# Attention with a channel mix on one core: the low parts of the weights subtracted on VectorE instead of GpSimd

## The chip, the cores and the metric

One core of one Trainium2 chip runs the whole program. The metric is the device time of one execution, in microseconds. Engines are named as in the profile: PE (TensorE matmul), PEld (its weight load), DVE (VectorE), ACT (ScalarE), POOL (GpSimd), SP (SyncE, which issues the loads and stores here).

## The reference

Four sequences of 768 tokens with 8 heads of 64 pass through attention with a window of 96 local and 8 global keys and a distance bias; its output, 512 wide, goes through a channel mix:

```python
xk = mu_k * x + (1.0 - mu_k) * x_prev      # x_prev: the token before
xr = mu_r * x + (1.0 - mu_r) * x_prev
k = np.maximum(xk @ w_k, 0.0)              # 512 x 1024
v = k * k @ w_v                            # 1024 x 512
r = 1.0 / (1.0 + np.exp(-(xr @ w_r)))      # 512 x 512
return (r * v).astype(np.float32)
```

The weights come as float64.

## The kernel before

The 3072 tokens are 24 tiles of 128 queries, and 12 chunks of two tiles. For each tile, attention runs in four pairs of heads: `scores` (PE s, L287 for the first seven tiles, L289 and L290 later; then DVE e with the bias and its extreme nmax, L295; ACT exp, L296; DVE r, L302 and L303; POOL e times r, L306), `transposes` (PE t, L317; ACT et, L318) and `weighted` (PE av, L334). The channel mix of a chunk begins three tiles after the chunk's first: `mix` makes xk and xr, each as a high and a low part (POOL or ACT, then DVE L358, ACT L359, DVE L360); then come the products kp with w_k (four banks of 24 matmuls), z with w_r (two of 12) and vps with w_v (two of 24), each as three products of high and low parts (L371 to L373). ACT and DVE square the positive part of kp in between (L397 to L400: kk, kk_hi, kk_lo); ACT makes the sigmoid of z (L405) and DVE multiplies it with vps (L414).

The weights are converted once, at the start, in 20 blocks of 128 x 512: eight of w_k, four of w_r, eight of w_v, in this order (numbers 0 to 19). `weight_begin` loads a block's float64 words (SP, L159) and builds its leading bits as a float32 `a`: ACT Abs (L166 or L169), POOL L167 for the first eight and DVE L170 for the rest, and DVE L171, L172, L173 for all. L174 rounds `a` to the high part hi, on ACT or, for every other pair of blocks, on POOL (whose copies have line L196). `weight_end` subtracts hi from `a`, which gives the low part lo (L180, on POOL). `a` lies in a buffer that a later block, a kk or a sig takes once the subtraction has read it.

Three things set the order. In the source, the tiles are woven with steps of the channel mix by a budget (L423 to L472), and the blocks are begun and ended by a count of slots (L463 to L466). Then the program is built with a scheduler that lays each engine's queue out ahead of time by a timeline of its own (L635), so a change on one engine can move rows on all. On the chip each engine runs its queue in order and waits only where a row's inputs or buffers aren't there. The PSUM banks of kp, z and vps are three (L80), taken in turn: kp, kp, kp, kp, z, z, vps, vps of a chunk, then the next chunk's; each waits until what reads the bank three before it is done. So the second kp of chunk 1 (kp_1270 below) waits for L414 of the first vps of chunk 0 (vps_1072). The pool `p4k` of three buffers (L67) holds the words of blocks 8 to 19, the mixes' sums, and the queries and keys of tiles from 7 on.

Of the kernel before, what the change touches and what calls it, by code (L numbers as in the profile page):

```python
# [9 lines left out]
F32 = mybir.dt.float32  # L10
# [9 lines left out]
B, H, S, D = 4, 8, 768, 64  # L20
# [1 line left out]
NT = S // 128  # L22
NTILES = B * NT
NCHUNK = NTILES // 2
NATIVE = 7  # first tiles, whose scores are plain float32 products
GMAX = 32
LMAX = 97
NEG = -1.0e9
FAR = 1.0e12
HUGE = (1.875 - 2.0**-13) * 2.0**32  # bits 0x4FEFFC00  # L30


@with_exitstack
def tile_biased_attention_channel_mix(ctx: ExitStack, tc: tile.TileContext, qT, kT, v, n_sizes, mu_kr, w_k, w_v, w_r, q_rows, k_rows, v_rows, slopes, out):
    nc = tc.nc
    vec, act, pool, pe = nc.vector, nc.scalar, nc.gpsimd, nc.tensor

    const = ctx.enter_context(tc.tile_pool(name="const", bufs=1))

# [1 line left out]
    sizes_w = const.tile([128, 2, 2], I32, name="sizes_w")  # L41
    nc.sync.dma_start(sizes_w.rearrange("p s w -> p (s w)"), n_sizes.partition_broadcast(128))
    words = const.tile([128, 2, 2], F32, name="words")
    sizes = const.tile([128, 2], F32, name="sizes")
# [13 lines left out]
    nc.scalar.dma_start(mus.rearrange("p a j -> p (a j)"), mu_kr)  # L58
    mu = {name: (mus[:, i, :], mus1[:, i, :]) for i, name in enumerate("kr")}

# [1 line left out]
    wts = {}  # L62
    for name, kts, n in (("k", 4, DF), ("r", 4, DM), ("v", 8, DM)):
        wts[name] = tuple(const.tile([128, kts, n], F32R, name=f"w{name}_{p}") for p in ("hi", "lo"))
# [14 lines left out]
    ps_a = fast.enter_context(tc.tile_pool(name="ps_a", bufs=1, space=PSUM))  # L79
    ps_f = fast.enter_context(tc.tile_pool(name="ps_f", bufs=3, space=PSUM))  # L80

    # the tensor engine's clock rises with use: products of zeros until the first tile is there
    zeros = const.tile([128, 512], BF16, name="zeros")
    vec.memset(zeros, 0.0)
    for i in range(10):
        idle = ps_f.tile([128, 512], F32, name="idle", tag="f")
        pe.matmul(idle, zeros[:, 0:128], zeros, start=True, stop=True)

# [1 line left out]
    # The distance; n_local for a key that is only global, which is over any distance of a local key;  # L90
    # FAR or more where masked: such a key's weight is exactly 0.
    pat = const.tile([128, H, 256], BF16, name="pat")
    pat0 = const.tile([128, H, 128], BF16, name="pat0")
    btmp = f_pool.tile([128, 2048], F32, name="btmp", tag="kk_hi")
# [7 lines left out]
    ints, flts, local, glo, dist0, dist = (piece() for _ in range(6))  # L102
    ints = ints.bitcast(I32)
    j = flts[:, 224:352]
    # 96 keys before the tile, then the tile's own
    pool.iota(ints[:, 96:224], [[-1, 128]], base=0, channel_multiplier=1)
    pool.iota(ints[:, 224:352], [[1, 128]], base=0, channel_multiplier=0)
    pool.iota(ints[:, 0:96], [[-1, 96]], base=96, channel_multiplier=1)
# [3 lines left out]
    vec.tensor_max(causal, causal, dist0)  # L112
    read_sizes()

    # tile 0
    vec.tensor_scalar(local[:, 96:224], causal, nlf, FAR, op0=ALU.is_ge, op1=ALU.mult)
    vec.tensor_scalar(glo, j, ngf, FAR, op0=ALU.is_ge, op1=ALU.mult)
    vec.tensor_add(local[:, 96:224], local[:, 96:224], causal)
# [5 lines left out]
        else:  # L124
            pool.tensor_scalar(pat0[:, h, :], dist0, c, 1.0, op0=ALU.mult, op1=ALU.mult)

    # later tiles: 32 keys from the start, 96 keys before the tile, the tile
    vec.tensor_scalar(local[:, 0:96], flts[:, 0:96], nlf, FAR, op0=ALU.is_ge, op1=ALU.mult)
    vec.tensor_copy(dist[:, 128:256], local[:, 96:224])
    vec.tensor_scalar(dist[:, 0:32], glo[:, 0:32], nlf, None, op0=ALU.max)  # L130
# [11 lines left out]
    w_live = {}  # L142

    def weight_begin(i):
        # A float64 weight's words: (sign, 11 exponent bits, 20 bits), (32 bits).
        # a: its first 24 significant bits as a float32; hi: a rounded to float32r; lo: the rest of a.
        name, src, k, c = w_steps[i]
        if name != "k":
            raw = p4k.tile([128, 512, 2], I32, tag="t4k", name=f"w64_{i}")
            a = f2_pool.tile([128, 512], I32, tag="f2", name=f"wa_{i}")  # L150
        elif k < 2:
            both = f_pool.tile([128, 2048], I32, tag=("kk_hi", "kk_lo")[k], name=f"w64_{i}")
            raw = both[:, 0:1024].rearrange("p (n w) -> p n w", w=2)
            a = both[:, 1024:1536]
        else:
            t = "xk" if k == 2 else "xr"
            raw = f_pool.tile([128, 512, 2], I32, tag=t + "_hi", name=f"w64_{i}")
            a = f_pool.tile([128, 512], I32, tag=t + "_lo", name=f"wa_{i}")
        nc.sync.dma_start(raw.rearrange("p n w -> p (n w)"), src[k * 128 : (k + 1) * 128, 2 * c : 2 * c + 1024])  # L159
        low, top = raw[:, :, 0], raw[:, :, 1]  # L160
        hi = wts[name][0][:, k, c : c + 512]
        # top's bits as a float32: times 2**-112 (or 2**16, which differs in a bit that the shift drops) moves the float64
        # exponent's bias to the float32's. What float32 cannot hold is bounded: from 2**128 up (by Inf, which stays Inf,
        # or the min) to a large number, under 2**-127 (by underflow or the max) to 0.
        if i < 8:
            act.activation(a.bitcast(F32), top.bitcast(F32), AF.Abs, scale=2.0**111)  # L166
            pool.tensor_scalar(a.bitcast(F32), a.bitcast(F32), 2.0**-112, 2.0**-111, op0=ALU.mult, op1=ALU.mult)  # L167
        else:
            act.activation(a.bitcast(F32), top.bitcast(F32), AF.Abs, scale=2.0**16)  # L169
            vec.tensor_scalar(a.bitcast(F32), a.bitcast(F32), 2.0, HUGE, op0=ALU.max, op1=ALU.min)  # L170
        vec.tensor_scalar(a, a, 3, 0x7FFFFFF8, op0=ALU.logical_shift_left, op1=ALU.bitwise_and)  # L171
        vec.scalar_tensor_tensor(a, top, -0x80000000, a, op0=ALU.bitwise_and, op1=ALU.bitwise_or)  # L172
        vec.scalar_tensor_tensor(a, low, 29, a, op0=ALU.logical_shift_right, op1=ALU.bitwise_or)  # L173
        (act.copy if i % 4 < 2 else pool_copy)(hi, a.bitcast(F32))  # L174
        w_live[i] = a

    def weight_end(i):
        name, src, k, c = w_steps[i]
        hi, lo = (w[:, k, c : c + 512] for w in wts[name])
        pool.tensor_sub(lo, w_live.pop(i).bitcast(F32), hi)  # L180

    w_count = [0, 0]

# [11 lines left out]
    def pool_copy(dst, src):  # L195
        pool.tensor_scalar(dst, src, 1.0, 1.0, op0=ALU.mult, op1=ALU.mult)  # L196

# [1 line left out]
    state = {}  # L199
    # the first tiles' queries and keys, with 64 rows of zeros: products of all 128 rows keep the tensor engine's clock up  # L200
    padded = []
    for i in range(2):
        qz = q_pool.tile([128, H, 128], F32, name=f"qz_{i}", tag="qh")
# [5 lines left out]
    def load_tile(n):  # L209
        b, t = divmod(n, NT)  # L210
        s = state[n] = {}
        native = n < NATIVE
        halves = (0,) if native else (0, 64)
        if native:
            qr, kr = padded[n % 2]
        else:
            qr = p4k.tile([128, H, 128], F32, tag="t4k", name=f"qraw_{n}")
            if n == NATIVE:
                kr = kw_pool.tile([128, H, 256], F32, tag="kw", name=f"kraw_{n}")
# [4 lines left out]
        for o in halves:  # L224
            if n <= NATIVE:
                nc.sync.dma_start(kr[o : o + 64, :, 128:256], kT[n])
# [13 lines left out]
        state[n]["va"] = va  # L240

    def global_v(n):
        # the tile before, now with the 32 first rows in place of its own
        b, t = divmod(n, NT)
        if t >= 2:
            nc.sync.dma_start(state[n - 1]["va"][0:32], v[b, 0:32, :])

    def split_tile(n):
# [4 lines left out]
        s["e"] = {}  # L253
        if n < NATIVE:
            return
        qh = q_pool.tile([128, H, 128], F32R, name=f"qh_{n}", tag="qh")
        ql = q_pool.tile([128, H, 128], F32R, name=f"ql_{n}", tag="ql")
        kw = kw_pool.tile([128, H, 256], F32R, name=f"kw_{n}", tag="kw")
        cur = kw[:, :, 0 if n == NATIVE and t else 128 : 256]
        kr = s["kr"]  # L260
        if n == NATIVE:
            kr = kr[:, :, 256 - cur.shape[2] : 256]
# [81 lines left out]
            xt = state["x", c]  # L344
            act.copy(xt[:, :, 1 + 128 * i : 129 + 128 * i], s["av"].rearrange("p (a q) -> p a q", a=4))

# [1 line left out]
    def mix(xc, xp, tag, tmp_pool, out_pool, on_act=False):  # L348
        m, m1 = mu[tag]
        tmp = tmp_pool.tile([128, 4, 256], F32, name=f"mix_{tag}", tag="t4k")  # L350
# [69 lines left out]
        xr = mix(xt[:, :, 1:257], xt[:, :, 0:256], "r", p4k, f_pool, c == 0)  # L420
        return channel_mix(xk, xr, lambda i: out[(2 * c + i) * 128 : (2 * c + i + 1) * 128, :], f_pool, f2_pool, ps_f)

# [1 line left out]
    LAG = 3  # tiles from a chunk's first to the start of its channel mix  # L424
    queue = []
    budget = [0.0]

# [13 lines left out]
    for step in range(NTILES + 1):  # L441
# [4 lines left out]
        for hp in range(4):  # L446
# [8 lines left out]
            if hp == 0:  # L455
                if step >= LAG and (step - LAG) % 2 == 0:
                    queue.append(ffn((step - LAG) // 2))
                    if len(queue) == 1 and step == LAG:
                        budget[0] = -17.5
# [12 lines left out]
        run_ffn(1.0)  # L472
    fast.close()

# [1 line left out]
    def wide():  # L476
        with ExitStack() as g:
            once = g.enter_context(tc.tile_pool(name="g_once", bufs=1))
# [7 lines left out]
            dist, keep = ([once.tile([128, S], F32, name=f"{n}_{t}") for t in range(NT)] for n in ("dist", "keep"))  # L486
# [9 lines left out]
            for t in range(NT):  # L496
                pool.iota(ji, [[-1, S]], base=t * 128, channel_multiplier=1)
                vec.tensor_copy(rel, ji)
                loc = keep[t]
                vec.tensor_scalar(loc, rel, 0.0, None, op0=ALU.is_ge)  # L500
                vec.tensor_scalar(tmp, rel, nlf, None, op0=ALU.is_lt)
                vec.tensor_mul(loc, loc, tmp)
                # only global: n_local; else the distance
                vec.tensor_sub(tmp, glob, loc)
                vec.tensor_scalar(tmp, tmp, 0.0, None, op0=ALU.max)
                vec.tensor_scalar(keep_n, tmp, nlf, None, op0=ALU.mult)
                vec.tensor_scalar(tmp, tmp, -1.0, 1.0, op0=ALU.mult, op1=ALU.add)
                vec.scalar_tensor_tensor(dist[t], rel, -1.0, rel, op0=ALU.mult, op1=ALU.max)
                vec.tensor_mul(dist[t], dist[t], tmp)
                vec.tensor_add(dist[t], dist[t], keep_n)  # L510
                vec.tensor_max(keep[t], loc, glob)
# [49 lines left out]
            rows = xs.rearrange("(b a p) s -> b p a s", b=B, p=128)  # L561
# [16 lines left out]
                    for _ in channel_mix(xk, xr, out_rows, work, work4, ps_f):  # L578
                        pass

    # 1 where the short windows do not hold every kept key
    okf = const.tile([128, 2], F32, name="okf")
    wide_i = const.tile([1, 1], I32, name="wide_i")
    vec.tensor_scalar(okf[:, 0:1], nlf, float(LMAX), None, op0=ALU.is_le)
# [54 lines left out]
```

## Time and profile before

| | |
|---|---|
| median of 3 runs | 525.55 us (525.51 to 526.01) |
| span of the profiled execution | 524.1 us |
| median less span | 1.45 us |
| PE busy | 495.9 us (95%) |
| DVE, ACT, POOL busy | 372.4, 323.6, 283.0 us |

The span is from the first to the last instruction of the one execution that the profiler took; its own time isn't given apart from the span, and the runs' median stands 1.45 us above it. Rows of the timeline begin with a start and a duration in us; in brackets stands how long the engine had been idle and what released it. Rows of groups end with busy time, the mean of one in ns, and the idle time ahead of them. Matmul rows overlap one another, so a matmul's cost is read from start to start.

### The profile page before, as it was taken

How to read it: one execution, taken by the hardware profiler on the slowest of the kernel's cores; microseconds unless marked ns; L12 is line 12 of the kernel's file. 1: busy time of each engine (PE TensorE's matmuls, PEld its weight loads, DVE VectorE, ACT ScalarE, POOL GpSimd, SP SyncE). 2: the span in 40 equal slices, each digit the busy share in tenths (PEclk: the TensorE clock that was granted, in tenths of full speed). 3: DMA queues.
4: the chain of work that ended last, by engine and by line, in shares of the span. 5: the costliest groups of instructions: out<-in, count | busy, mean ns of one | idle time of the engine just before them, and what ended most of it. 6: DMA issues, size and time to landing. Idle time of an engine off the chain costs nothing.

```text
span 524.1 us, 9900 instructions
## 1 busy us (share of the span) xinstructions
PE 495.9 (95%) x3466; PEld 427.2 (82%) x3466; DVE 372.4 (71%) x854; ACT 323.6 (62%) x730; POOL 283.0 (54%) x410
## 2 busy tenths in 40 slices
PE   7885888979999999999999999999999999999995
PEld 4563766869898898898898898898898898898984
DVE  6799999987677766767767867767777865535321
ACT  4868585823957856846847757756757667643220
POOL 8799977987355644544547645535547634203000
PEclk9979799999999999999999999999999999999999
DMA  8998268150350530530521431521422210000101
GB/s 197 322 232 198 67 185 188 41 144 20 107 134 6 141 107 5 157 91 8 162 76 38 130 86 34 133 86 59 124 62 66 62 46 26 35 12 2 41 1 44
DMA packets 27304, 48.16 MB, mean 92 GB/s; under 512 B 7216, under 2 KB 13360, under 8 KB 27248
## 3 DMA queue, kind: packets, MB, share of 16 engines
q1 hardware_dynamic: 27104, 47.46, 34.0%
q8 instruction: 29, 0.48, 0.4%
q14 instruction: 27, 0.22, 0.1%
q10 hardware_dynamic: 144, 0.00, 0.0%
HBM read 41.16 MB, written 6.29 MB: 91 GB/s over the span
## 4 chain that ended last, share of the span: by engine, by line
PE 80%; DVE 11%; POOL 5%; issue 3%; DMA 1%; ACT 0%; DVEq 0%; POOLq 0%
PE vps L372 8%; PE vps L373 8%; PE vps L371 8%; PE kp L371 8%; PE kp L373 8%; PE kp L372 8%; PE av L334 7%; PE t L317 6%; PE z L371 4%; PE z L373 4%; PE z L372 4%; PE s L290 3%; PE s L289 3%; POOL e L306 2%; PE s L287 2%
## 5 line engine op out<-in xcount | busy, mean ns | idle before, releaser
L306 POOL TENSOR_SCALAR e<-e,r 128x256 f32<-128x256 f32 (+1 forms) x192 | 106.1, 570 | 137.0 <-DVE r L303 91.9
L371 PE MATMUL kp<-xk_hi,wk_hi 128*128 128x256 f32 x384 | 108.0, 282 | 0.2 <-DVE kk L398 0.2
L373 PE MATMUL kp<-xk_hi,wk_lo 128*128 128x256 f32 x384 | 107.5, 280 | 0.5 <-POOL wk_lo L180 0.5
L372 PE MATMUL kp<-xk_lo,wk_hi 128*128 128x256 f32 x384 | 107.3, 279 | 0.0
L296 ACT ACTIVATE e<-e,nmax 128x256 f32<-128x256 f32 (+1 forms) x192 | 92.6, 484 | 22.0 <-DVE nmax L295 21.0
L295 DVE CUSTOM_DVE_ANT_0 e<-s,pat 128x256 f32<-128x256 f32 (+1 forms) x192 | 69.0, 395 | 31.0 <-PE s L290 21.2
L372 PE MATMUL vps<-wv_lo,kk_hi 128*128 128x512 f32 x192 | 76.0, 396 | 2.6 <-POOL wv_lo L180 2.6
L371 PE MATMUL vps<-wv_hi,kk_hi 128*128 128x512 f32 x192 | 75.9, 395 | 0.4 <-POOL wv_hi L196 0.4
L373 PE MATMUL vps<-wv_hi,kk_lo 128*128 128x512 f32 x192 | 75.8, 395 | 0.0
L371 PEld LDWEIGHTS kp<-xk_hi,wk_hi 128*128 128x128 f32 x384 | 72.9, 190 | 1.2 <-DVE kk L398 0.6
L373 PEld LDWEIGHTS kp<-xk_hi,wk_lo 128*128 128x128 f32 x384 | 72.8, 190 | 0.9 <-POOL wk_lo L180 0.9
L372 PEld LDWEIGHTS kp<-xk_lo,wk_hi 128*128 128x128 f32 x384 | 72.9, 190 | 0.6
L318 ACT COPY et<-t 128x512 f32<-128x512 f32 (+1 forms) x96 | 52.0, 546 | 20.2 <-PE t L317 19.7
L317 PE MATMUL t<-ident,e 128*128 128x128 f32 x352 | 57.5, 280 | 5.7 <-POOL e L306 5.6
L398 DVE TENSOR_TENSOR kk<-kp,kk 128x512 f32<-128x512 f32 x48 | 33.1, 689 | 41.2 <-ACT kk L397 41.0
L317 PEld LDWEIGHTS t<-ident,e 128*128 128x128 f32 x352 | 41.2, 141 | 19.1 <-POOL e L306 9.2
L334 PE MATMUL av<-et,va 128*64 128x128 f32 x704 | 49.4, 284 | 0.6 <-ACT et L318 0.6
L334 PEld LDWEIGHTS av<-et,va 128*64 128x64 f32 x704 | 40.3, 139 | 10.5 <-issue 5.8
L400 DVE TENSOR_TENSOR kk_lo<-kk,kk_hi 128x512 fp32r<-128x512 f32 x48 | 35.3, 735 | 17.4 <-ACT kk_hi L399 17.3
L399 ACT CAST kk_hi<-kk 128x512 fp32r<-128x512 f32 x48 | 29.8, 622 | 25.6 <-DVE kk L398 25.6
L397 ACT ACTIVATE kk<-kp 128x512 f32<-128x512 f32 x48 | 28.3, 590 | 26.7 <-PE kp L373 24.5
L372 PEld LDWEIGHTS vps<-wv_lo,kk_hi 128*128 128x128 f32 x192 | 36.0, 187 | 10.5 <-POOL wv_lo L180 3.1
(103 smaller groups left out, 1051.1 us busy)
## 6 DMA issues: line engine op xcount, KB each, us to landing
kraw<-in_kT_dram SPq DMA_DIRECT2D x36, 256.0 KB, 3.9
qraw<-in_qT_dram SPq DMA_DIRECT2D x34, 256.0 KB, 4.1
va<-in_v_dram SPq DMA_DIRECT2D x24, 256.0 KB, 3.1
out_dram<-sig SPq DMA_DIRECT2D x24, 256.0 KB, 3.5
w<-in_w_k_dram SPq DMA_DIRECT2D x8, 512.0 KB, 9.1
w<-in_w_v_dram SPq DMA_DIRECT2D x8, 512.0 KB, 3.5
kz<-in_kT_dram SPq DMA_DIRECT2D x8, 256.0 KB, 6.7
w<-in_w_r_dram SPq DMA_DIRECT2D x4, 512.0 KB, 9.3
```

The lines of the kernel that those rows point to most:

```text
L295: vec.tensor_tensor_reduce(out=e[:, :w], in0=o, in1=p[:, h, :], op0=ALU.add, op1=ALU.min, scale=-0.125, scalar=3.0e38, accum_out=s["nmax"] ...
L296: act.activation(e[:, :w], e[:, :w], AF.Exp, bias=s["nmax"][:, h : h + 1], scale=-1.0, accum_out=s["sum"][:, h : h + 1])
L306: pool.tensor_scalar(e[:, :w], e[:, :w], r[:, u : u + 1], 1.0, op0=ALU.mult, op1=ALU.mult)
L317: pe.transpose(pt[:, c : c + 128], e[:, k * 128 : (k + 1) * 128], ident)
L318: act.copy(et[:, : 2 * nb * 128], pt[:, : 2 * nb * 128])
L334: pe.matmul(o, vt[:, h * 64 : (h + 1) * 64], et[:, c : c + 128], start=k == 0, stop=k == nb - 1)
L371: pe.matmul(o, sh, mh, start=first, stop=False)
L372: pe.matmul(o, sh, ml, start=False, stop=False)
L373: pe.matmul(o, sl, mh, start=False, stop=last)
L398: vec.tensor_mul(kk, pv, kk)
L399: act.copy(kkh[:, 2 * fp : 2 * fp + 2, :], kk)
L400: vec.tensor_sub(kkl[:, 2 * fp : 2 * fp + 2, :], kk, kkh[:, 2 * fp : 2 * fp + 2, :])
```

## The change

Line 180, in `weight_end`, names another engine:

```diff
-        pool.tensor_sub(lo, w_live.pop(i).bitcast(F32), hi)
+        vec.tensor_sub(lo, w_live.pop(i).bitcast(F32), hi)
```

The comments go too, and line numbers stay. The scheduler lays the queues out anew, up to the eighth tile; from tile 8 on the queues of DVE and PE are the same as before.

On POOL, the 20 subtractions leave. This is the first half of w_k (rows with - were there before):

```order
 L306 TENSOR_SCALAR e_6_386<-e_6_386,r_3_392 128x256
 L306 TENSOR_SCALAR e_7_389<-e_7_389,r_3_392 128x256
-L180 TENSOR_TENSOR wk_lo<-wa_239,wk_hi 128x512
-L180 TENSOR_TENSOR wk_lo<-wa_258,wk_hi 128x512
 L306 TENSOR_SCALAR e_0_437<-e_0_437,r_1_469 128x256
 L306 TENSOR_SCALAR e_1_440<-e_1_440,r_1_469 128x256
 L306 TENSOR_SCALAR e_2_463<-e_2_463,r_1_469 128x256
 L306 TENSOR_SCALAR e_3_466<-e_3_466,r_1_469 128x256
-L180 TENSOR_TENSOR wk_lo<-w_0_203,wk_hi 128x512
-L180 TENSOR_TENSOR wr_lo<-wa_400,wr_hi 128x512
```

They stood between the bursts of four e; now the bursts follow one another. On DVE, the end of the weights before, from the last step of block 18 (wa_939) and block 19 (wa_989) to the two L414 of chunk 0 (xk, xr and mix belong to chunk 1, ql_1351 to tile 7):

```order
 L173 SCALAR_TENSOR_TENSOR wa_939<-w_18_938,wa_939 128x512
 L360 TENSOR_TENSOR xk_lo<-mix_k,xk_hi 128x1024
 L172 SCALAR_TENSOR_TENSOR wa_989<-w_19_988,wa_989 128x512
 L358 SCALAR_TENSOR_TENSOR mix_r<-x_746,mus,mix_r 128x256 x2
 L173 SCALAR_TENSOR_TENSOR wa_989<-w_19_988,wa_989 128x512
 L358 SCALAR_TENSOR_TENSOR mix_r<-x_746,mus,mix_r 128x256 x2
 L360 TENSOR_TENSOR xr_lo<-mix_r,xr_hi 128x1024
 L265 TENSOR_TENSOR ql_1351<-qraw_1206,qh_1350 128x1024
 L414 TENSOR_TENSOR sig<-vps,sig 128x512 x2
 L295 ISA e_6_1422,nmax_1122<-s_3_1419,pat_141 128x128
```

And the same place now:

```order
 L360 TENSOR_TENSOR xk_lo<-mix_k,xk_hi 128x1024
 L173 SCALAR_TENSOR_TENSOR wa_939<-w_18_938,wa_939 128x512
 L173 SCALAR_TENSOR_TENSOR wa_989<-w_19_988,wa_989 128x512
 L358 SCALAR_TENSOR_TENSOR mix_r<-x_746,mus,mix_r 128x256 x4
 L180 TENSOR_TENSOR wv_lo<-wa_939,wv_hi 128x512
 L180 TENSOR_TENSOR wv_lo<-wa_989,wv_hi 128x512
 L360 TENSOR_TENSOR xr_lo<-mix_r,xr_hi 128x1024
 L398 TENSOR_TENSOR kk<-kp,kk 128x512
 L265 TENSOR_TENSOR ql_1351<-qraw_1206,qh_1350 128x1024
 L414 TENSOR_TENSOR sig<-vps,sig 128x512
 L265 TENSOR_TENSOR ql_1580<-qraw_1452,qh_1579 128x1024
 L414 TENSOR_TENSOR sig<-vps,sig 128x512
```

The last two subtractions and chunk 1's first kk stand ahead of the first L414 now, and tile 6's last e (e_6_1422 and its neighbour) and tile 7's kw have moved ahead of these rows. On PE, the place of tile 6's transposes (t_6) before, behind all of chunk 1's kp and in its second z:

```order
 L373 MATMUL z_1408<-wr_hi_72,xr_lo_1052 128x512
 L334 MATMUL av_5_1460<-et_5_3_1413,va_5_1000 64x128
 L334 MATMUL av_5_1460<-et_5_3_1413,va_4_727 64x128
 L334 MATMUL av_5_1460<-et_5_3_1413,va_5_1000 64x128
 L317 MATMUL t_6_0_1478<-ident_62,e_6_0_1247 128x128
 L371 MATMUL z_1445<-wr_hi_72,xr_hi_1051 128x512
 L372 MATMUL z_1445<-wr_lo_73,xr_hi_1051 128x512
```

And now, where the first kp of chunk 1 (kp_1193) begins; the second, kp_1270, follows some rows on, behind two score products of tile 7:

```order
 L334 MATMUL av_6_1679<-et_6_1_1540,va_6_1214 64x128 x2
 L372 MATMUL vps_1072<-wv_lo_75,kk_hi_698 128x512
 L373 MATMUL vps_1072<-wv_hi_74,kk_lo_699 128x512
 L372 MATMUL vps_1141<-wv_lo_75,kk_hi_698 128x512
 L373 MATMUL vps_1141<-wv_hi_74,kk_lo_699 128x512
 L317 MATMUL t_6_2_1588<-ident_62,e_6_4_1367 128x128
 L317 MATMUL t_6_2_1588<-ident_62,e_6_5_1370 128x128
 L371 MATMUL kp_1193<-xk_hi_1038,wk_hi_70 128x256
 L317 MATMUL t_6_3_1622<-ident_62,e_6_6_1422 128x128
 L317 MATMUL t_6_3_1622<-ident_62,e_6_7_1425 128x128
```

Tiles 5 and 6 stand earlier on PE, ahead of chunk 1's second kp.

## The prediction

> **What bounds the kernel now.** I read a table of busy time by stages first (busy us and count of PE, PEld, DVE, ACT, POOL, then granted clock, DMA share, GB/s), then who waits for whom on PE, then the timelines of DVE and POOL side by side. The two stages that matter are the 104 us in which the weights are converted and the long one after it.
>
> ```profile
> 13.00:117.00 104.00, 84.79 (x531) 65.55 (x532) 98.16 (x222) 68.86 (x178) 89.12 (x103) 0.93 0.67 171
> 117.00:510.00 393.00, 393.00 (x2877) 349.11 (x2874) 264.57 (x587) 249.12 (x534) 183.37 (x287) 1.00 0.25 69
> ```
>
> From 117 to 510 us PE is busy all 393.00 us, so no edit to another engine can shorten that stretch. In the stage before it PE is idle 104.00 - 84.79 = 19.2 us, and there DVE (98.16 of 104) and POOL (89.12) are nearly full. All 20 weight blocks are converted there. The end of the kernel moves by as much as PE's full stretch begins earlier or later with a given amount of work behind it. PE's waits in this stage, for 13 to 117 us:
>
> ```profile
> PE s L287 <- DVE nmax L295: 5.8, 2, 3.2
> PE t L317 <- POOL e L306: 5.6, 10, 1.2
> PE vps L372 <- POOL wv_lo L180: 2.6, 2, 1.8
> ```
>
> PE waits for DVE and for POOL; POOL's e waits in turn for DVE's r. So DVE's queue is the path, and its last part also runs through the subtractions on POOL. The last gap is this one, behind the last wv_lo:
>
> ```profile
> 114.58 0.50 PE L372 MATMUL vps<-wv_lo,kk_hi 128*128 128x512 f32 x1 [0.88 <-POOL wv_lo L180]
> ```
>
> **What the subtractions cost now.** Groups on POOL, 13 to 117 us:
>
> ```profile
> L306 POOL TENSOR_SCALAR e<-e,r 128x256 f32<-128x256 f32 (+1 forms) x52 | 37.9, 744 | 9.9 <-DVE r L303 8.8 <-DVE nmax L295 1.1
> L180 POOL TENSOR_TENSOR wv_lo<-wa,wv_hi 128x512 fp32r<-128x512 f32 x8 | 13.3, 1657 | 0.2
> L180 POOL TENSOR_TENSOR wr_lo<-wa,wr_hi 128x512 fp32r<-128x512 f32 x4 | 6.0, 1494 | 0.1
> L180 POOL TENSOR_TENSOR wk_lo<-w,wk_hi 128x512 fp32r<-128x512 f32 x4 | 5.9, 1468 | 0.0
> L180 POOL TENSOR_TENSOR wk_lo<-wa,wk_hi 128x512 fp32r<-128x512 f32 x4 | 5.3, 1343 | 0.1
> ```
>
> That is 13.3 + 6.0 + 5.9 + 5.3 = 30.5 us of POOL's 89.12. They cost DVE time as well. Here are the first and the last of 18 places where a DVE instruction is stretched while an L180 runs on POOL; each POOL row stands ahead of its DVE row.
>
> ```profile
> 31.43 2.71 POOL L180 TENSOR_TENSOR wk_lo<-wa,wk_hi 128x512 fp32r<-128x512 f32 x2
> 31.44 2.98 DVE L170 TENSOR_SCALAR wa<-wa 128x512 f32<-128x512 f32 x2
> 112.31 2.23 POOL L180 TENSOR_TENSOR wv_lo<-wa,wv_hi 128x512 fp32r<-128x512 f32 x1
> 113.30 2.32 DVE L265 TENSOR_TENSOR ql<-qraw,qh 128x1024 fp32r<-128x1024 f32 x1
> ```
>
> What the same DVE lines take undisturbed is the first of their three figures (min/median/max, ns); L400 has the form of the moved instruction:
>
> ```profile
> L170 DVE TENSOR_SCALAR wa<-wa x12: 393/746/1561, 27.3 to 102.3; 128x512 f32<-128x512 f32 x12
> L171 DVE TENSOR_SCALAR wa<-wa x16: 391/478/856, 20.3 to 103.3; 128x512 int32<-128x512 int32 x16
> L173 DVE SCALAR_TENSOR_TENSOR wa<-w,wa x16: 677/740/1773, 23.1 to 108.2; 128x512 int32<-128x512 int32 x16
> L358 DVE SCALAR_TENSOR_TENSOR mix_k<-x,mus,mix_k x48: 474/694/1527, 44.0 to 480.7; 128x256 f32<-128x256 f32 x48
> L302 DVE TENSOR_SCALAR r<-sum x48: 152/171/1220, 11.5 to 456.1; 128x4 f32<-128x4 f32 x48
> L400 DVE TENSOR_TENSOR kk_lo<-kk,kk_hi x48: 662/693/1784, 84.9 to 503.7; 128x512 fp32r<-128x512 f32 x48
> ```
>
> In the first place two L170 take 2.98 instead of some 0.75 us, a stall of 2.2; in the last, 2.32 instead of 1.28 (twice an L400's work), 1.0. Summed over the 18 places this is **18.4 us**. How much DVE stalls in all follows from the groups' means, 13 to 117 us:
>
> ```profile
> L173 DVE SCALAR_TENSOR_TENSOR wa<-w,wa 128x512 int32<-128x512 int32 x16 | 15.1, 948 | 0.0
> L172 DVE SCALAR_TENSOR_TENSOR wa<-w,wa 128x512 int32<-128x512 int32 x16 | 12.6, 795 | 0.1
> L170 DVE TENSOR_SCALAR wa<-wa 128x512 f32<-128x512 f32 x12 | 10.4, 874 | 0.0
> L171 DVE TENSOR_SCALAR wa<-wa 128x512 int32<-128x512 int32 x16 | 8.5, 535 | 0.0
> L358 DVE SCALAR_TENSOR_TENSOR mix_r<-x,mus,mix_r 128x256 f32<-128x256 f32 x8 | 7.2, 932 | 0.4 <-POOL mix_r L357 0.4
> L358 DVE SCALAR_TENSOR_TENSOR mix_k<-x,mus,mix_k 128x256 f32<-128x256 f32 x8 | 6.9, 882 | 0.0
> L171 DVE TENSOR_SCALAR w<-w 128x512 int32<-128x512 int32 x4 | 3.3, 820 | 1.0 <-POOL w L167 1.0
> L302 DVE TENSOR_SCALAR r<-sum 128x4 f32<-128x4 f32 x12 | 4.0, 332 | 0.0
> L400 DVE TENSOR_TENSOR kk_lo<-kk,kk_hi 128x512 fp32r<-128x512 f32 x4 | 4.0, 1005 | 0.0
> ```
>
> Busy time less count times the undisturbed figure (L172 with L173's): 4.3 + 1.8 + 5.7 + 2.2 + 3.4 + 3.1 + 1.6 + 2.2 + 1.4 = 25.7, and 1.0 for the L265 above: 27 us. So 18.4 of 27 us stand beside L180, and some 8.6 beside all other POOL work, which is spread over the 96 instructions of these groups: 0.09 us each.
>
> **The change as a sum on DVE's queue.** I follow DVE to the first multiply of L414, because in the new order its release of a PSUM bank is what PE meets last before its full stretch (kp_1270 takes the bank of the first vps). Before, these rows stand there; nothing held PE at that kp:
>
> ```profile
> 115.53 1.27 DVE L414 TENSOR_TENSOR sig<-vps,sig 128x512 f32<-128x512 f32 x2
> 117.96 0.39 PE L371 MATMUL kp<-xk_hi,wk_hi 128*128 128x256 f32 x1
> ```
>
> 1. The stalls beside L180 go: **-18.4**. Bounds: all of it, or none if other POOL work takes L180's place in time.
> 2. Twenty subtractions come: DVE starts the next instruction some 0.60 us after one of 0.66 to 0.69: 20 x 0.60 = **+12.0**.
> 3. They stall behind the POOL work that is left. As the rest of DVE does: 20 x 0.09 = 1.8. As L173 does with all its stalls: 20 x 0.27 = 5.4. I take 1.8, since L180 itself is gone, and 0.8 for one long POOL copy that is now met (the 1.91 below, at less than half): **+2.6**.
> 4. The new order puts other DVE work ahead of that L414 which was behind it: the kw subtraction (2.35 below, some 2.3), one L398 (0.6) and the last two heads of tile 6 with their r (0.6): **+3.5**.
> 5. DVE's two idle moments in its last stretch are filled by the moved work, 0.38 + 1.12: **-1.5**.
>
> ```profile
> 116.67 1.91 POOL L196 TENSOR_SCALAR kw<-kraw 128x2048 fp32r<-128x2048 f32 x1 [2.14 <-PE s L287]
> 120.44 2.35 DVE L266 TENSOR_TENSOR kw<-kraw,kw 64x2048 fp32r<-64x2048 f32 x1
> 106.95 1.31 DVE L358 SCALAR_TENSOR_TENSOR mix_r<-x,mus,mix_r 128x256 f32<-128x256 f32 x2 [0.38 <-POOL mix_r L357]
> 111.92 1.45 DVE L360 TENSOR_TENSOR xr_lo<-mix_r,xr_hi 128x1024 fp32r<-128x1024 f32 x1 [1.12 <-ACT xr_hi L359]
> ```
>
> The sum is -1.8: L414 starts at 113.7 and, at half of its row's 1.27, is done by 114.4; kp_1270 starts there instead of at 117.96: -3.6. PE then also has more behind it: eight transposes of tile 6, its eight products with v and two score products of tile 7 stand ahead of kp_1270 now and stood behind it before; at 0.12 us a transpose and 0.07 a product with v from the rows below, and a score product taken as a transpose, an estimate of 8 x 0.12 + 8 x 0.07 + 2 x 0.12 = 1.7. Together **-5.3 us**.
>
> ```profile
> 86.46 1.09 PE L317 MATMUL t<-ident,e 128*128 128x128 f32 x8
> 116.51 1.52 PE L334 MATMUL av<-et,va 128*64 128x128 f32 x22
> ```
>
> SP's loads of the weights wait for buffers that a subtraction or an L173 frees. Their order among the other loads changes little, and DMA has room for a load that comes later, at a share of 0.67 in this stage; I cost that at nothing, and if the cover fails it is the second rival or the third. On POOL 30.5 us leave; POOL is not what PE meets last then, so this counts only through earlier e and hi. Queued behind the moved subtraction on DVE are the scores of the next tile and the r of the last; behind its wait for hi (ACT or POOL) they would be held too, but the new order sets other blocks' work between. The span is 524.1, the median 525.55; the 1.45 us around the span I leave as they are. Forecast: 525.55 - 5.3 = 520.3 us.
>
> A rule that speaks against step 3: the Trainium skill, "SBUF — State Buffer", section "Who interferes with whom", says that a VectorE instruction with two SBUF inputs and a GpSimd instruction that reads SBUF exclude each other for a whole instruction, and the moved subtraction is such an instruction. By it alone a moved subtraction would meet POOL busy in (89.12 - 30.5) / 104 = 0.56 of cases and wait half an L306, 0.37 us: 20 x 0.21 = 4.2 instead of 1.8, and the sum would be 2.4 us worse, -2.9. The 18 stretched places agree with the rule; the 0.09 us per instruction beside other POOL work is under it.
>
> **The rivals.** *The stalls move instead of going.* DVE is full, so what no longer meets an L180 may meet an L306 or a hi copy. If half of the 18.4 comes back, the sum is -5.3 + 9.2 = +3.9: 529.5. It decides from 5.3 us on, under a third. For it: L306 has 37.9 us in this stage. Against: an L306 lasts 0.74 against 1.5, and comes in bursts while DVE does L295, which shows no stretch beside it. Chance 0.14.
>
> *Another wait takes the place.* The second vps needs a bank that the sigmoids free; these stand on ACT behind the last weight blocks' Abs, which wait for buffers that the subtractions free. Before, the pair ran here:
>
> ```profile
> 100.78 1.09 ACT L405 ACTIVATE sig<-z 128x512 f32<-128x512 f32 x2
> ```
>
> Should it end some 6 us later, at 108, PE has gained nothing: within 1 us of 525.5. Chance 0.12.
>
> *More goes.* With a third of its work gone, POOL may also stall DVE less elsewhere: half of the 8.6, -4.3, would make 516.0. There the loads of tile 7's queries hold it, which SP can issue only after xk_lo, as now:
>
> ```profile
> SPq L223 <- DVE xk_lo L360: 13.3, 1, 13.3
> ```
>
> Chance 0.12. That the change is not made is excluded: the order shows the 20 rows on DVE.
>
> **How the numbers follow.** The first case, all of it faster, has 0.62 and by the bounds of step 3, nothing or 5.4 + 0.8, its own range is 517.5 to 524. A measurement of this kernel tells about 0.2%, 1 us, from no change. Faster: 0.62 + 0.12 = 0.74; same 0.12; slower 0.14. The range of 516.0 to 526.5 takes in the first case, no change and the upper half of "more goes"; it leaves out most of the 0.14 and half of the last 0.12.
>
> **What would show it.** Right: DVE's L170, L171, L173 and L358 means in the first 117 us near their undisturbed figures, L180 on DVE at 0.66 to 0.8 us, and PE's full stretch from about 113 us on, with its idle time before that some 4 to 5 us less. Wrong: L180 on DVE over 1 us, L306 beside stretched DVE rows, or a PE gap behind ACT's sig or behind a kw or q load after 114 us.

## The result, and the profile after

The changed kernel takes 520.59 us (median of four runs, 519.92 to 521.01) against 525.64 us for the kernel before (four runs, 525.51 to 526.01): a ratio of 0.9894, with a 95% interval of 0.9882 to 0.9906. Its profiled execution is the shortest of the four: 519.92 us, with a span of 518.1.

The table by stages of the changed kernel, in the columns used before:

```profile
13.00:117.00 104.00, 87.10 (x592) 67.56 (x592) 98.26 (x247) 72.97 (x188) 70.58 (x92) 0.96 0.70 175
117.00:510.00 393.00, 393.00 (x2838) 349.04 (x2837) 261.71 (x581) 246.00 (x523) 175.86 (x278) 1.00 0.25 69
```

POOL has 18.5 us less to do in the first 117 us, DVE is exactly as full as before (98.26 and 98.16), and PE is busy 2.3 us longer. DVE's groups, 13 to 117 us:

```profile
L172 DVE SCALAR_TENSOR_TENSOR wa<-w,wa 128x512 int32<-128x512 int32 x16 | 13.2, 837 | 0.0
L173 DVE SCALAR_TENSOR_TENSOR wa<-w,wa 128x512 int32<-128x512 int32 x16 | 11.5, 728 | 0.0
L180 DVE TENSOR_TENSOR wv_lo<-wa,wv_hi 128x512 fp32r<-128x512 f32 x8 | 7.6, 964 | 0.0
L171 DVE TENSOR_SCALAR wa<-wa 128x512 int32<-128x512 int32 x16 | 6.8, 432 | 0.0
L170 DVE TENSOR_SCALAR wa<-wa 128x512 f32<-128x512 f32 x12 | 5.6, 469 | 2.5 <-ACT wa L169 2.5
L358 DVE SCALAR_TENSOR_TENSOR mix_r<-x,mus,mix_r 128x256 f32<-128x256 f32 x8 | 4.9, 638 | 0.7 <-POOL mix_r L357 0.7
L358 DVE SCALAR_TENSOR_TENSOR mix_k<-x,mus,mix_k 128x256 f32<-128x256 f32 x8 | 4.8, 630 | 0.0
L180 DVE TENSOR_TENSOR wk_lo<-wa,wk_hi 128x512 fp32r<-128x512 f32 x4 | 3.4, 842 | 0.0
L180 DVE TENSOR_TENSOR wr_lo<-wa,wr_hi 128x512 fp32r<-128x512 f32 x4 | 3.3, 825 | 0.0
L180 DVE TENSOR_TENSOR wk_lo<-w,wk_hi 128x512 fp32r<-128x512 f32 x4 | 3.1, 782 | 0.0
```

Busy time less count times the undisturbed figure gives 2.4 + 0.7 + 0.5 + 0.9 + 1.1 + 1.0 = 6.6 us for L172, L173, L171, L170 and the two L358. Before, these six groups had 20.5. So the stalls did go. The subtractions themselves take 7.6 + 3.4 + 3.3 + 3.1 = 17.4 us, which is 4.2 over 20 x 0.66: 0.21 us of stall each.

Where PE's full stretch begins, on DVE and then on PE:

```profile
114.28 0.68 DVE L398 TENSOR_TENSOR kk<-kp,kk 128x512 f32<-128x512 f32 x1
116.26 0.68 DVE L414 TENSOR_TENSOR sig<-vps,sig 128x512 f32<-128x512 f32 x1
115.02 0.38 PE L371 MATMUL kp<-xk_hi,wk_hi 128*128 128x256 f32 x1 [0.31 <-DVE kk L398]
```

The kp at 115.02 is kp_1270. It starts 2.9 us earlier than before, and ahead of the L414 that was to release its bank: it waits for L398. In the new layout the pool gives it the bank of kp_1193 (5), not that of vps_1072 (7). In the kernel before the three banks do go round in turn (7, 6, 5); in the new program the turn is broken at this one place.

From kp_1270 to the first transposes of tile 7 (from which on both queues are the same), PE took 149.39 - 117.96 = 31.4 us before and takes 143.47 - 115.02 = 28.5 now. Here are the two ends, of before and then of after:

```profile
149.39 0.65 PE L317 MATMUL t<-ident,e 128*128 128x128 f32 x4
```

```profile
143.47 0.60 PE L317 MATMUL t<-ident,e 128*128 128x128 f32 x4
```

That is 2.9 + 3.0 = 5.9 us; the last L414 stands 6.0 us earlier. PE's waits changed their kind; 13 to 140 us, after:

```profile
PE t L317 <- POOL e L306: 10.5, 11, 1.8
PE av L334 <- ACT et L318: 1.7, 3, 1.0
```

The 5.8 us behind nmax, the 2.6 behind the low parts and the 2.3 behind kk are gone, but the waits for POOL's e have grown from 5.6 to 10.5, although POOL has less to do.

### The profile page after: what moved, and what is told of

Its sections match the earlier page's. It is cut to its first block, busy times and chain, and to the rows that moved or that the text cites. A ratio compares the mean times of both kernels' runs of the same rounds, so it can differ in the third digit from the quotient of the medians.

```text
span 518.1 us, 9916 instructions
## 1 busy us (share of the span) xinstructions
PE 491.0 (95%) x3466; PEld 423.6 (82%) x3466; DVE 368.9 (71%) x874; ACT 324.6 (63%) x730; POOL 257.0 (50%) x390
## 5 line engine op out<-in xcount | busy, mean ns | idle before, releaser
L306 POOL TENSOR_SCALAR e<-e,r 128x256 f32<-128x256 f32 (+1 forms) x192 | 106.4, 571 | 148.6 <-DVE r L303 88.1
L295 DVE CUSTOM_DVE_ANT_0 e<-s,pat 128x256 f32<-128x256 f32 (+1 forms) x192 | 69.0, 395 | 33.1 <-PE s L290 24.4
L317 PE MATMUL t<-ident,e 128*128 128x128 f32 x352 | 57.2, 279 | 10.7 <-POOL e L306 10.5
L398 DVE TENSOR_TENSOR kk<-kp,kk 128x512 f32<-128x512 f32 x48 | 33.0, 688 | 41.1 <-ACT kk L397 40.9
L317 PEld LDWEIGHTS t<-ident,e 128*128 128x128 f32 x352 | 40.9, 141 | 24.1 <-POOL e L306 15.1
L334 PE MATMUL av<-et,va 128*64 128x128 f32 x704 | 48.5, 282 | 2.7 <-ACT et L318 1.7
L334 PEld LDWEIGHTS av<-et,va 128*64 128x64 f32 x704 | 39.5, 138 | 12.0 <-issue 4.9
L373 PEld LDWEIGHTS vps<-wv_hi,kk_lo 128*128 128x128 f32 x192 | 36.0, 187 | 8.7
L371 PEld LDWEIGHTS vps<-wv_hi,kk_hi 128*128 128x128 f32 x192 | 35.9, 187 | 8.7 <-ACT sig L405 1.0
```

Of the source, the lines that this page charges most:

```text
L295: vec.tensor_tensor_reduce(out=e[:, :w], in0=o, in1=p[:, h, :], op0=ALU.add, op1=ALU.min, scale=-0.125, scalar=3.0e38, accum_out=s["nmax"] ...
L306: pool.tensor_scalar(e[:, :w], e[:, :w], r[:, u : u + 1], 1.0, op0=ALU.mult, op1=ALU.mult)
L317: pe.transpose(pt[:, c : c + 128], e[:, k * 128 : (k + 1) * 128], ident)
L334: pe.matmul(o, vt[:, h * 64 : (h + 1) * 64], et[:, c : c + 128], start=k == 0, stop=k == nb - 1)
L371: pe.matmul(o, sh, mh, start=first, stop=False)
L373: pe.matmul(o, sl, mh, start=False, stop=last)
```

## The experiments

Three theories: **A**, the gain is DVE's stalls beside the subtractions (the prediction's); **B**, it is POOL's shorter queue; **C**, it is the new order of the queues. All stretch or shrink the same stage, so the order had to be held. In most runs below each engine's rows are chained in the order in which they stand in one of the two kernels, the table `order`; a chained row is only issued behind the one ahead, it doesn't wait for its end:

```diff
+    for n, own_i in enumerate(order):
+        for i in [own_i] + [names[a] for a in behind.get(n, [])]:
+            if i.engine in last:
+                tc.add_manual_dep(i, last[i.engine], mybir.DependencyInfo(mybir.DependencyClass.NoSync, mybir.DependencyReason.DATA))
+            last[i.engine] = i.name
```

`behind` holds added rows. The PSUM banks are then those of that kernel too. "The old order" is that of the kernel before, "the new order" that of the changed one.

### Engine or order

Old order, L180 on DVE:

```diff
-        pool.tensor_sub(lo, w_live.pop(i).bitcast(F32), hi)
+        vec.tensor_sub(lo, w_live.pop(i).bitcast(F32), hi)
```

> The queues of PE, DVE, ACT, POOL and SP are held in the order of the kernel before, and so are the PSUM banks; only the 20 subtractions of L180 stand on DVE, each at its old place in time. Theory A (the engine: DVE no longer stalls beside the subtractions on POOL, 18.4 us, and that is more than their 12 us and their own stalls on DVE): most of the gain without the new order, 520 to 523.5 us. Theory B (POOL's load: its queue is 30 us shorter, so e and hi come earlier): also faster, 520 to 524. Theory C (the new order of the queues is what gained): no gain, 525 to 530, since DVE then carries 12 us more in an order laid out without them.

Measured: 517.49 us, ratio to before 0.9838 (0.9821 to 0.9855), faster than either theory gave and 3.1 us faster than the changed kernel. Its waits of PE, 13 to 140 us:

```profile
PE t L317 <- POOL e L306: 6.3, 10, 1.2
PE s L287 <- DVE nmax L295: 3.6, 4, 1.4
```

New order, L180 on POOL (the same line the other way):

> The order and the PSUM banks of the changed kernel, with the 20 subtractions back on POOL at their places in time. Theory A: the stalls beside them return on DVE's old rows (some 18 us) while 12 + 4 us leave DVE, so the time goes back most of the way, 523 to 527 us. Theory B: the same, POOL's queue is long again, 523 to 527. Theory C: the order is kept, so the time stays at 520 to 521.5.

Measured: 529.00 us, ratio 1.0051 (1.0037 to 1.0065), slower than every theory gave. PE's first wait:

```profile
PE t L317 <- POOL e L306: 15.4, 15, 3.6
```

The four corners: 525.83 and 517.49 us in the old order (POOL, DVE), 529.00 and 520.59 in the new. The engine is worth 8.3 or 8.4 us, and the new order costs 3.2 or 3.1, whichever of the two is changed first. C as a source of the gain falls; the order is a cost, and it shows as PE waiting for e.

### POOL's queue with and without reads

The changed kernel in its new order, with more work on POOL where the subtractions had stood; `patf` is the bias table's memory taken as float32. With reads:

```diff
+    ADDED.extend([pool.tensor_sub(spare, patf[:, 0:4, :], patf[:, 4:8, :]).ins.name] for n in range(20))
```

> The changed kernel in its own order, with 20 more subtractions on POOL that read two float32 rows of 512 from SBUF (of the bias table) and write bfloat16 that nobody reads, at the places where the subtractions stood in the run before this one. DVE keeps its own 20. Theory A: DVE's old rows and its L180 stall again, 18 to 24 us in all, over half of it on the path: 532 to 542 us. Theory B: POOL's queue is as long as before the change and nothing else: 522 to 526. Theory C: little, 520 to 523.

Measured: 536.71 us, ratio 1.0206 (1.0187 to 1.0224). Without reads:

```diff
+    ADDED.extend([pool.memset(spare, 0.0).ins.name for u in range(4)] for n in range(20))
```

> As the run with the added reads, but POOL only writes: 80 memsets of 128x384 float32 in groups of four at the same places, about as long in all as the 20 subtractions were (to be read from the profile), with no read of SBUF. Theory A: no DVE row beside a memset is stretched, so the time stays within 2 us of the changed kernel, 520 to 522.5 us, what is lost being e that comes later. Theory B (POOL's load): the gain is given back, 524 to 527 us. Between this run and the one with reads, A expects 10 us or more, B under 2.

Measured: 532.04 us, ratio 1.0109 (1.0087 to 1.0131). L182 is the added line. Groups of 13 to 117 us (L180 and L295 to 125) and PE's first wait, of the run with reads and then of the run without:

```profile
L182 POOL TENSOR_TENSOR spare<-pat 128x512 bf16<-128x512 f32 x18 | 28.0, 1554 | 0.2
L180 DVE TENSOR_TENSOR wk_lo<-wa,wk_hi 128x512 fp32r<-128x512 f32 x4 | 5.2, 1308 | 0.0
PE t L317 <- POOL e L306: 20.1, 18, 3.7
```

```profile
L182 POOL MEMSET spare<- 128x384 f32 x72 | 32.0, 444 | 3.3
L180 DVE TENSOR_TENSOR wk_lo<-wa,wk_hi 128x512 fp32r<-128x512 f32 x4 | 2.7, 678 | 0.7 <-POOL wk_hi L196 0.7
L295 DVE CUSTOM_DVE_ANT_0 e<-s,pat 128x256 f32<-128x256 f32 (+1 forms) x48 | 17.2, 391 | 7.0 <-PE s L287 4.2 <-PE t L317 2.8
PE t L317 <- POOL e L306: 16.9, 13, 3.1
```

A is right about the stretching: in the first half of w_k a subtraction on DVE takes 0.678 us beside memsets and 1.308 beside reading POOL work; over the 18 that lie in the stage the means are 0.68 and 1.01 us. But A's time for the memsets is wrong by some 10 us: with no subtraction stretched, 80 x 0.444 = 35.5 us of memsets cost 532.04 - 520.59 = 11.45 us of the end, 0.32 us each. B's 524 to 527 us is missed too, by 5 us: the memsets take more than the whole gain back. POOL's queue is on the path, DVE now sits idle behind PE (7.0), and of the 16.1 us that the reads cost, 20 x 1.554 = 31.1 us at 0.32 make 10.0. The other 6.1 are left for the stalls. One DVE row does run longer beside these memsets: L171 takes 569 ns after 432, 2.2 us in its 16 rows, and a part of the 11.45 may be that.

The same memsets in the old order:

> The old order with the subtractions on DVE (517.49 us), and 80 memsets of 128x384 on POOL, four at each place where a subtraction stood: POOL's queue is as long as before the change, yet nothing on it reads SBUF there. Theory A (most of the 8.3 us came from DVE rows no longer stretched beside the subtractions): 517 to 521 us. Theory B (most came from POOL's shorter queue, e reaching PE earlier): 523 to 528 us. If both have a share, the time stands between, and the distance from 517.49 is POOL's share.

Measured: 528.88 us, ratio 1.0051 (1.0034 to 1.0068). That is 11.39 us for 80 x 0.441 = 35.3 us of memsets: 0.32 again, with L171 no longer than without them (500 ns after 512). It is slower than before the change and just past B's range, so B's share is real in either order.

### The stalls and the subtractions, each by itself

Old order, the low parts set to zero on POOL, in about the subtractions' time:

```diff
-        pool.tensor_sub(lo, w_live.pop(i).bitcast(F32), hi)
+        w_live.pop(i); zero = [pool.memset(lo.bitcast(F32)[:, 0:m], 0.0).ins.name for m in (512, 512, 256)]
```

> The old order; each subtraction on POOL is replaced by three memsets of its low part there (512, 512 and 256 columns, some 1.5 us together), so the low parts of the weights are zero and the products with them add nothing. POOL's queue stays about as long as before, no DVE row stands beside a subtraction, and DVE has no subtraction either. Theory A: DVE loses 18 us of stall and takes nothing on, so this is faster than with the subtractions on DVE: 511 to 517 us. Theory B: POOL's queue sets the end, so little is gained: 523 to 526 us. The distance between this run and the one before it is what 20 subtractions cost on DVE: 12 to 16 us of its queue, of which A expects 4 to 8 in the time and B under 2.

Measured: 517.58 us, ratio 0.9833 (0.9816 to 0.9849). The stage in the table, and POOL's groups in it:

```profile
13.00:117.00 104.00, 92.94 (x605) 72.51 (x604) 87.83 (x230) 72.42 (x187) 94.72 (x149) 0.94 0.70 176
```

```profile
L180 POOL MEMSET wk_lo<- 128x512 f32 (+1 forms) x24 | 11.9, 500 | 0.9
L180 POOL MEMSET wv_lo<- 128x512 f32 (+1 forms) x24 | 11.6, 484 | 0.9
L180 POOL MEMSET wr_lo<- 128x512 f32 (+1 forms) x12 | 5.9, 493 | 0.5
```

These 29.4 us stand for the 30.5 of the subtractions, so POOL's load is about the same and the mutual stalls are gone: 526.00 - 517.58 = 8.4 us less. Not all of it need be the stalls: a memset reads neither `a` nor hi, so the buffer of `a` comes free earlier (ACT's Abs waited 2.6 us for wv_lo in the kernel before, and not at all here), and no run separates the two. DVE is idle 104.00 - 87.83 = 16.2 us here, where it was 5.8: its rows lose 15 us of stall (the prediction's nine groups have 10.7 left of 25.7), and 10.3 us come back as its own waiting for PE, POOL and ACT. The time lies just past A's range of 511 to 517, and far from B's. Then with one memset of 512 columns each (4.5 + 4.1 + 2.1 = 10.7 us):

> The old order as in the run with the low parts set to zero (517.58 us), but one memset of 512 columns each in place of three: POOL's memsets go from 29.4 us to some 10 to 12. Low parts are zero again. If taking a microsecond off POOL's queue gains what putting one on costs (11.4 us of the end for 34.4 us of memsets, 0.33 each): 517.58 - 18 x 0.33 = 511.6, so 510 to 513.5 us. If the queue was the path only when it was made longer: 515 to 518.

Measured: 511.65 us, ratio 0.9727 (0.9711 to 0.9744): 5.93 us less for 18.7 us less of POOL, 0.32 each. Taking POOL's load away gains what adding it costs.

```profile
L180 POOL MEMSET wv_lo<- 128x512 f32 x8 | 4.5, 558 | 0.0
L180 POOL MEMSET wk_lo<- 128x512 f32 x8 | 4.1, 524 | 0.0
L180 POOL MEMSET wr_lo<- 128x512 f32 x4 | 2.1, 523 | 0.0
```

Old order with L180 on DVE, and 20 more subtractions on DVE:

```diff
+    ADDED.extend([vec.tensor_sub(spare, patf[:, 0:4, :], patf[:, 4:8, :]).ins.name] for n in range(20))
```

> The old order with the subtractions on DVE (517.49 us), and behind each of them one more subtraction on DVE of the same form (two float32 inputs from the bias table, bfloat16 out, read by nobody). That is 20 x 0.6 to 0.85 = 12 to 17 us more on DVE's queue. Theory A (DVE's queue sets when PE's full stretch begins): over half of it reaches the end, 525 to 533 us. Theory B (POOL's queue does): 518 to 522 us.

Measured: 528.73 us, ratio 1.0048 (1.0031 to 1.0065). The added group:

```profile
L182 DVE TENSOR_TENSOR spare<-pat 128x512 bf16<-128x512 f32 x19 | 14.4, 758 | 0.0
```

20 x 0.758 = 15.2 us of DVE cost 11.24 us of the end, 0.74 each. In the old order L180 itself has 6.2 + 3.1 + 3.1 + 3.0 = 15.4 us on DVE. So the engine's move can be added up from single prices: stalls (and earlier buffers) -8.4, POOL's queue -30.5 x 0.32 = -9.8, DVE's queue +15.4 x 0.74 = +11.4; together -6.8, where the move measured -8.3. The 1.5 us between are open: the prices were taken one at a time, on kernels that differ.

The clock granted to PE was not held either. In the stage of 13 to 117 us it is 0.95 in the old order with L180 on DVE, but 0.91 with the memsets added and 0.89 with the second subtractions. What that is worth can be estimated from the kernel before, whose executions were measured beside these runs: those with a mean clock of 0.970 to 0.977 took 0.6 to 1.1 us longer in the mean than those with 0.979 to 0.989. So a microsecond or so of the 11.39 and of the 11.24 may be the clock's, and the prices of added work are upper bounds by that much. The step from three memsets to one has 0.94 on both sides, and the 0.32 stands there without it.

### The pairs of instructions by themselves

The kernel's work is replaced by streams of these forms, in stages that begin on both engines together:

```python
vec.tensor_sub(out_d, src_d[0], src_d[1])
vec.tensor_scalar(out_d, src_d[0], mark[:, 0:1], 1.0, op0=ALU.mult, op1=ALU.add)
vec.scalar_tensor_tensor(out_d, wide_d[:, :, 0], mark[:, 0:1], src_d[0], op0=ALU.mult, op1=ALU.add)
pool.memset(out_p, 0.0)
pool.tensor_scalar(out_p[:, 0:256], src_p[0][:, 0:256], mark[:, 1:2], 1.0, op0=ALU.mult, op1=ALU.mult)
pool.tensor_sub(out_p, src_p[0], src_p[1])
```

> Only pairs of instructions, none of the kernel's work; the output is filled with the last sums. Twelve stages one after the other: 24 DVE instructions of one form (two float32 inputs of 128x512; one input; two inputs of which one is every second word, as in L172) beside nothing, beside 24 POOL memsets of 128x512, beside 24 POOL products of 128x256 with a column (the form of L306), beside 12 POOL subtractions of 128x512 (the form of L180); then the three POOL forms alone. Theory A (a POOL instruction that reads SBUF holds every DVE form, and a DVE instruction holds it): no DVE form is longer beside memsets; all three are longer beside the other two, by 0.15 us or more in the mean beside the subtractions; POOL's products take 0.37 us alone and 0.6 or more beside DVE. Rival (only DVE's forms with two inputs are held): the one-input form stays at its time of some 0.35 us beside all three.

DVE's stages on the timeline, for each of two forms beside nothing, memsets, products and subtractions:

```profile
5.12 17.34 DVE L53 TENSOR_TENSOR out_d<-src_d,src_d 128x512 f32<-128x512 f32 x24
23.22 17.40 DVE L53 TENSOR_TENSOR out_d<-src_d,src_d 128x512 f32<-128x512 f32 x24
41.44 21.01 DVE L53 TENSOR_TENSOR out_d<-src_d,src_d 128x512 f32<-128x512 f32 x24
63.26 28.69 DVE L53 TENSOR_TENSOR out_d<-src_d,src_d 128x512 f32<-128x512 f32 x24
92.77 12.50 DVE L56 TENSOR_SCALAR out_d<-src_d,mark 128x512 f32<-128x512 f32 x24
106.09 17.85 DVE L56 TENSOR_SCALAR out_d<-src_d,mark 128x512 f32<-128x512 f32 x24
124.76 14.60 DVE L56 TENSOR_SCALAR out_d<-src_d,mark 128x512 f32<-128x512 f32 x24
140.17 23.25 DVE L56 TENSOR_SCALAR out_d<-src_d,mark 128x512 f32<-128x512 f32 x24
```

POOL's: subtractions beside the two-input form, memsets beside the one-input form, and the three forms alone:

```profile
63.28 20.13 POOL L62 TENSOR_TENSOR out_p<-src_p,src_p 128x512 f32<-128x512 f32 x12
...
106.08 17.58 POOL L68 MEMSET out_p<- 128x512 f32 x24
...
255.85 6.92 POOL L68 MEMSET out_p<- 128x512 f32 x12
263.25 6.76 POOL L65 TENSOR_SCALAR out_p<-src_p,mark 128x256 f32<-128x256 f32 x12
270.48 16.00 POOL L62 TENSOR_TENSOR out_p<-src_p,src_p 128x512 f32<-128x512 f32 x12
```

A POOL subtraction takes 11.35 / 12 = 0.95 us from a two-input DVE stream and 10.75 / 12 = 0.90 from a one-input one, an L306 product 0.15 and 0.09; the form with every second word is held as the two-input form is (29.63 beside subtractions, 18.86 alone and beside memsets). So the rival falls: the one-input form is held too. A falls in one place: memsets leave two-input DVE alone (17.40) but not the one-input form, 17.85 against 12.50. Its 0.37 us for an L306 product alone was too low as well: 0.56.

The Trainium skill, "SBUF — State Buffer", section "Who interferes with whom", says that a two-input VectorE instruction contends with a GpSimd instruction that reads SBUF, not with one that only writes, and that a tensor_scalar in a two-port mode contends with either; the rows agree on all three, if the one-input form here runs in such a mode, which they don't show by themselves. It also says that one blocks the other for the whole instruction. For two subtractions the rows nearly say so: after POOL's 20.13 us DVE still had 91.95 - 83.41 = 8.5 us of work left, 11.8 of its 24; so 12 DVE and 12 POOL subtractions shared the time at 20.13 / 12 = 1.68 us a pair, where 0.72 + 1.33 would be 2.05. For a subtraction beside an L306 product they don't: 21.01 / 24 = 0.88 us a pair, where 0.72 + 0.56 would be 1.28.

### Versions that go further

Old order, L180 on DVE, and all high parts on ACT:

```diff
-        (act.copy if i % 4 < 2 else pool_copy)(hi, a.bitcast(F32))
+        act.copy(hi, a.bitcast(F32))
```

> The old order with the subtractions on DVE (517.49 us), and the ten high parts that POOL rounds (L174 by L196, 7.7 us in all) on ACT, at 0.62 us each. Theory A: ten fewer POOL rows that read SBUF beside DVE, each worth at most half a microsecond of stall: 515.5 to 517.5 us. Theory B: e comes some microseconds earlier in places: 514 to 516.5 us. Rival: ACT's exp and copies are held behind the ten copies, 518 to 520 us.

Measured: 515.62 us, ratio 0.9800 (0.9780 to 0.9820). 7.7 us less on POOL at 0.32 is 2.5; measured 1.9. Then also the first eight L167 on DVE:

```diff
-        if i < 8:
+        if i < 0:
```

> The old order with the subtractions on DVE and the high parts on ACT (515.62 us), and the first eight blocks' L167 on DVE as L170 (with the scale and bounds of the other twelve): POOL loses 8 x 0.85 = 6.8 us, DVE takes 8 x 0.34 to 0.5 = 2.7 to 4. Theory A and B together (one microsecond on DVE's queue cost 0.65 us of the end before, one on POOL's 0.33, in these runs): +1.8 to +2.6 for DVE, -2.2 for POOL, and fewer stalls: 514 to 516.5 us. Rival: DVE's queue alone is the path now, 517 to 519.

Measured: 514.20 us, ratio 0.9771 (0.9758 to 0.9785), the fastest complete version here: 6.4 us under the changed kernel. The edit of the first of these two, with L180 on DVE, and no order held:

> Subtractions on DVE and high parts on ACT, and the scheduler lays the queues out itself. If the new order of the changed kernel is a cost of 3 us that any layout with the subtractions on DVE brings: 518 to 520 us. If the order is a matter of chance from one version to the next: anywhere from 513 to 523.

Measured: 524.92 us (ten runs, 522.87 to 526.07), ratio 0.9971 (0.9957 to 0.9986): 9.3 us slower than the same instructions on the same engines in the old order, and above both forecasts. Its waits of PE, 13 to 150 us:

```profile
PE t L317 <- POOL e L306: 6.5, 5, 2.0
PE s L287 <- DMA kz<-in_kT_dram: 4.5, 2, 3.5
PE t L317 <- ACT et L318: 2.6, 1, 2.6
```

The layout sets a load of keys and a copy of transposes late. In the two layouts that the scheduler made anew the order costs 3.1 and 9.3 us, the second more than the change is worth. Why a layout comes out as it does, no run shows.

## Why the prediction was right

The forecast of 520.3 us met 520.59, in size and in sign. That it met within 0.3 us is in part luck: by the four corners the change is 8.3 us won by the engine less 3.1 lost by the new order, and the prediction's sum was made of other terms, some of whose errors cancel.

- **Step 1 (stalls beside L180 go, -18.4)**: right on DVE's queue. The nine groups of the prediction have 8.1 us of stall left of 25.7, and L265's 1.0 is gone. For the end it is worth 8.4 at most (the run with zeros): the prediction took DVE's queue as never waiting, and freed of the stalls it waits 10.3 us more in that run.
- **Step 2 (+12.0)**: right; L180 on DVE reaches down to 0.65 us where nothing holds it.
- **Step 3 (+2.6)**: too small. A subtraction stalls 0.21 us, not 0.09: 4.2 in all, within the bounds of 1.8 and 5.4. The 4.2 that the prediction worked out from the rule of the Trainium skill ("SBUF — State Buffer", "Who interferes with whom") is what was measured, though the pairs above hold one another for less than a whole instruction. The 0.09 came from rows of many forms. Why the moved one stalls more isn't shown; two inputs alone don't explain it, since L173 has two and keeps 0.7 / 16 = 0.04 us.
- **Step 4 (+3.5)**: its rows do stand ahead (L266 at 95.3 us, L398 at 114.3). The order that puts them there costs 3.1 us of the end.
- **Step 5 (-1.5)**: failed. Of the two idle moments the 1.12 ahead of xr_lo went, the 0.38 ahead of mix_r grew to 0.73, and another of 2.5 us came ahead of 86.7, behind ACT's Abs (the L170 row above), which waited for its block's words:

```profile
86.03 0.66 ACT L169 ACTIVATE wa<-w 128x512 f32<-128x512 f32 x1 [3.00 <-DMA w<-in_w_v_dram]
```

  DVE's idle time in the stage is 5.7 us after 5.8.
- **The sum to L414**: first L414 at 116.26, not at 113.7. **The PSUM bank** was the wrong one: kp_1270 waited for L398, 2.0 us ahead of L414 on DVE's queue. The two errors leave kp_1270 at 115.02, 0.6 late.
- **PE's work behind it (-1.7)**: -3.0, mis-sized. Summed from start to start between kp_1270 and tile 7's transposes, before has 1.62 us of products with v, 0.53 of transposes and 0.57 more of scores than after, and kp and z take 0.27 us more around them. The prediction took one row of L334, 0.07 us, for one product; a product has two, for each transposed block is multiplied once, and L334 has twice the rows of L317 in the kernel before:

```profile
L317 PE MATMUL t<-ident,e 128*128 128x128 f32 x352 | 57.5, 280 | 5.7 <-POOL e L306 5.6
L334 PE MATMUL av<-et,va 128*64 128x128 f32 x704 | 49.4, 284 | 0.6 <-ACT et L318 0.6
```

  And three products of tile 5 moved along with tile 6's eight. The transposes were priced too high (0.96 for 0.53); some 0.8 us of the 3.0 are places where the form changes (last section).
- **POOL's 30.5 us, costed at nothing**: this is the step that failed. "POOL is not what PE meets last then" looked at one place; over the whole stage e's way runs through DVE's r and POOL's L306, and each microsecond on POOL is worth 0.32 of the end: 9.8. What was left out there is, by luck, about what was counted too much for the stalls, 18.4 - 8.4 = 10.0.
- **The rivals.** Stalls moving instead of going: L306 takes 762 ns in the mean, 744 before, and the moved work meets 4.2 us, less than its 5.3. Another wait: the sigmoids ran at 98.48 and 101.56, the second behind a subtraction (1.95 us), and PE waited 0.6 us for the first. More goes: not by its mechanism; but the old order would have given 517.5.
- **What hides what**: the order of SP's loads, costed at nothing, was not harmless: DVE's 2.5 us of step 5 stand behind a load of words. What they cost the end isn't known. In the version laid out freely PE itself waited 4.5 us for keys.

The profiled span fell by 6.0 and the median by 5.05; the profiled execution is the shortest of its four.

## What to carry to other kernels

Where two engines pass work to and fro (DVE's r, POOL's e, PE's transposes), price a microsecond on each by adding a known load to it, before an engine is written off as not on the path: here DVE's cost up to 0.74 and POOL's 0.32 of the end, and stalls between the two up to another 8.4. With a scheduler that lays the queues out anew, hold the order while you measure an edit, and then hold a good one: the same 8.3 us edit showed as 5.1, and a further gain of 1.9 as a loss of 4.3. Compare the granted clock of the stage as well; holding the order did not hold it here (0.89 to 0.95). Last, look up which bank or buffer a row really waits for in the new program; a pool need not go round in the order of the source.

## What the runs showed of the hardware

- A one-input tensor_scalar of 128x512 on DVE (0.52 us alone, back to back) takes 0.74 beside POOL memsets, and they 0.73 instead of 0.58; two-input forms don't notice memsets.
- POOL is held as DVE is: L306's form takes 6.76 / 12 = 0.56 us alone and 0.89 beside two-input DVE (21.32 for 24). In the kernel it takes 0.76 in this stage.
- A transpose or a product with v among other products costs PE some 0.08 us where the form changes, which no wait shows. In the kernel before, behind a transpose, the row after the first product starts 0.20 us later, and the next one 0.12:

```profile
135.83 0.36 PE L289 MATMUL s<-kw,qh 128*128 128x256 f32 x1
136.03 0.28 PE L290 MATMUL s<-kw,ql 128*128 128x256 f32 x1
136.15 0.28 PE L289 MATMUL s<-kw,qh 128*128 128x256 f32 x1
```

Before, nine such places lie from kp_1270 to tile 7's transposes, 0.9 us together; after, one of 0.1, at kp_1270's own start. A change from kp to a score without a transpose costs nothing: in the changed kernel these rows start at 117.83, 117.94 and 118.06.
